# Rewriting a fused convolution-and-mixer kernel: a two-stage odd-frequency DFT with exchanges through DRAM, a row-form mixer with DMA transposes, and one list of tasks

## The chip, the cores and the metric

The kernel runs on one core of one Trainium2 chip. The time is the device time of one execution in microseconds (us); each figure is the median of several executions of the same program. The kernel before took 506.17 us (four runs, 503.19 to 508.12).

The engines are named as the profile names them: PE (TensorE, matmuls), PEld (its weight loads), DVE (VectorE), ACT (ScalarE), POOL (GpSimd) and SP (SyncE, which here issues every DMA). Matmul results land in PSUM; in these kernels DVE or ACT copies ("evicts") them to on-chip memory (SBUF).

## The reference, cut to what matters

Sequence S = 2048, width D = 640, hidden F = 1536, all bf16. Two branches read the same input `x = A_q` and are mixed by a gate per row.

```python
# branch A: a 4-tap causal filter, then a convolution as long as the sequence
k_shift = sum over t of pad(k)[t : t+S] * shift_k[:, 3-t]
kv      = k_shift * v
y       = irfft(rfft(pad(kv)) * rfft(pad(ssm_k)))[:S].astype(bf16)
y       = y + kv * ssm_D
a       = q * y
# branch B: a mixer that moves channel groups in time
h   = gelu(layernorm(x) @ w1)                          # 640 -> 640
h   = 4 groups of 160 channels, moved by 1, -1, 2, -2 rows
x1  = x + h @ w2
b   = x1 + gelu(layernorm(x1) @ w3) @ w4               # 640 -> 1536 -> 640
g   = sigmoid((x * gate_w).sum(-1))
out = g * a + (1 - g) * b
```

## The kernel before

It is four blocks of work, one after the other. (1) Tables of sines are generated on DVE and ACT. (2) The mixer runs in column form: `x` is transposed on its way in from DRAM, channels lie on the partitions, the means of the layernorm come from matmuls with a matrix of ones, and gelu is four operations, two of them on DVE reading PSUM. (3) The filter `k*v` runs on DVE, row block by row block. (4) The long convolution is cut into 4 blocks of 512 rows. Each block is transformed by a dense DFT matrix, every pair of blocks is multiplied on DVE, and each block is transformed back.

```python
NBLK = 4
...
def gelu_to(ps, writes):
    nc.scalar.activation(out=sq[:], in_=ps, func=ACT.Square, scale=float(np.sqrt(GELU_C)))
    nc.vector.scalar_tensor_tensor(out=uu[:], in0=sq[:], scalar=1.0, in1=ps, ...)      # L223
    nc.scalar.activation(out=sg[:], in_=uu[:], func=ACT.Sigmoid, scale=GELU_K)         # L226
    for (oap, r0, cnt) in writes:
        nc.vector.tensor_tensor(out=oap, in0=sg[r0:r0 + cnt], in1=ps[r0:r0 + cnt], op=ALU.mult)  # L228
...
for c in range(SC):                       # mixer, second half: 4 chunks of 512 rows
    X1N = normalize(XT, c)
    for ft in range(FT):                  # 12 tiles of W3, five matmuls each
        ...
        gelu_to(ps[:], [(GT[:, ft, :], 0, P)])
    for uu in range(SUB):                 # W4, plus an identity matmul that adds x1 back
        ...
for u in range(ST):                       # k*v: eight DVE operations of 640 columns per row block
    ...
    for j in (2, 1, 0):
        nc.vector.tensor_tensor(out=tmp[:], in0=KJ[:, j, :], in1=CJ[:, j, :], op=ALU.mult)  # L355
        nc.vector.tensor_tensor(out=acc[:], in0=acc[:], in1=tmp[:], op=ALU.add)             # L356
...
for i in range(NBLK):                     # convolution
    fwd_transform([KV[:, i * LT + tt, :] for tt in range(LT)], XSP[:], 1.0)
    for kblk in range(i, NBLK):
        for qt in range(LT):              # six or eight DVE operations of 128 x 640 each (L393)
            tt_op(t1[:], Xc, Hc, ALU.mult)
            tt_op(t2[:], Xs, Hs, ALU.mult)
            ...
    for m in range(LT):                   # inverse transform (L459), gate, result
        ...
```

Of the kernel before, what the change touches and what calls it, by code (L numbers as in the profile page):

```python
# [13 lines left out]
I32 = mybir.dt.int32  # L14

NBLK = 4
GELU_K = 1.5957691216057308
GELU_C = 0.044715
# [3 lines left out]
def kernel(  # L22
# [17 lines left out]
    P = nc.NUM_PARTITIONS  # L40

    _, S, D = A_q.shape
    Fh = B_w3.shape[1]
    assert S % (NBLK * P) == 0 and D % P == 0 and Fh % P == 0
    ST = S // P
    DT = D // P
    FT = Fh // P
    NCH = min(512, S)
    assert S % NCH == 0
    SC = S // NCH  # L50
    SUB = NCH // P
    L = S // NBLK
    LT = L // P
    M2 = 2 * L
    CG = D // 4
    shifts = [1, -1, 2, -2]
    NF = CG // P
    R = CG % P
    assert R in (0, 32, 64)
    assert 4 * NF * P + 4 * R == D  # L60

    def nchunks(n, c=512):
        res = []
        o = 0
        while o < n:
            w = min(c, n - o)
            res.append((o, w))
            o += w
        return res

    DCH = nchunks(D)

    q2 = A_q.rearrange("b s d -> (b s) d")
    k2 = A_k.rearrange("b s d -> (b s) d")
    v2 = A_v.rearrange("b s d -> (b s) d")
    out2 = out.rearrange("b s d -> (b s) d")

    consts = ctx.enter_context(tc.tile_pool(name="consts", bufs=1))
    persist = ctx.enter_context(tc.tile_pool(name="persist", bufs=1))
    kpool = ctx.enter_context(tc.tile_pool(name="kpool", bufs=1))  # L80

    KV = persist.tile([P, ST, D], BF16, name="KV")
    T2 = persist.tile([P, ST, D], BF16, name="T2")
    G32 = persist.tile([P, ST], F32, name="G32")
    OMG32 = persist.tile([P, ST], F32, name="OMG32")

    DBC = consts.tile([P, D], BF16, name="DBC")
    nc.sync.dma_start(out=DBC[:], in_=A_ssm_D.partition_broadcast(P))
    GWT = consts.tile([P, DT], BF16, name="GWT")
    with nc.allow_non_contiguous_dma(reason="gate weight transpose (tiny)"):  # L90
        nc.sync.dma_start(out=GWT[:], in_=gate_w.rearrange("(dt p) -> p dt", p=P))
    GWC = consts.tile([P, DT], F32, name="GWC")
    nc.vector.tensor_copy(out=GWC[:], in_=GWT[:])
    CJB = consts.tile([P, D * 4], BF16, name="CJB")
    nc.sync.dma_start(out=CJB[:], in_=A_shift_k.rearrange("d j -> (d j)").partition_broadcast(P))
    CJ = consts.tile([P, 4, D], BF16, name="CJ")
    CJBv = CJB.rearrange("p (d j) -> p d j", j=4)
    for j in range(4):
        nc.vector.tensor_copy(out=CJ[:, j, :], in_=CJBv[:, :, j])
    ONES = consts.tile([P, P], BF16, name="ONES")  # L100
    nc.vector.memset(ONES[:], 1.0)
    EPS = consts.tile([P, 1], F32, name="EPS")
    nc.vector.memset(EPS[:], 1e-5)
    CROUND = float(2 ** 23 + 2 ** 22)
    BL = consts.tile([P, 1], F32, name="BL")
    nc.vector.memset(BL[:], float(L))
    BZ = consts.tile([P, 1], F32, name="BZ")
    nc.vector.memset(BZ[:], 0.0)
    BC = consts.tile([P, 1], F32, name="BC")
    nc.vector.memset(BC[:], CROUND)  # L110
    BM = consts.tile([P, 1], F32, name="BM")
    nc.vector.memset(BM[:], -2.0 * M2 * CROUND)

    basis = ctx.enter_context(tc.tile_pool(name="basis", bufs=1))
    FW = basis.tile([P, 2, LT, L], BF16, name="FW")
    SIN_SCALE = np.pi * (1 - 2.0 ** -20) / M2

    def gen_basis(gen_pool, dst, kt, ncols, row_is_t):
        GC = min(ncols, 512)
        irow = gen_pool.tile([P, 1], I32, name="irow")  # L120
        if row_is_t:
            nc.gpsimd.iota(irow[:], pattern=[[1, 1]], base=P * kt, channel_multiplier=1)
        else:
            nc.gpsimd.iota(irow[:], pattern=[[1, 1]], base=2 * P * kt + 1, channel_multiplier=2)
        frow = gen_pool.tile([P, 1], F32, name="frow")
        nc.vector.tensor_copy(out=frow[:], in_=irow[:])
        for col0 in range(0, ncols, GC):
            icol = gen_pool.tile([P, GC], I32, name="icol")
            if row_is_t:
                nc.gpsimd.iota(icol[:], pattern=[[2, GC]], base=2 * col0 + 1, channel_multiplier=0)  # L130
            else:
                nc.gpsimd.iota(icol[:], pattern=[[1, GC]], base=col0, channel_multiplier=0)
            fcol = gen_pool.tile([P, GC], F32, name="fcol")
            nc.vector.tensor_copy(out=fcol[:], in_=icol[:])
            for comp in range(2):
                n1 = gen_pool.tile([P, GC], F32, name="n1")
                nc.vector.tensor_scalar(out=n1[:], in0=fcol[:], scalar1=frow[:], scalar2=float(L if comp == 0 else 0),
                                        op0=ALU.mult, op1=ALU.add)
                qq = gen_pool.tile([P, GC], F32, name="qq")
                nc.vector.tensor_scalar(out=qq[:], in0=n1[:], scalar1=1.0 / (2 * M2), scalar2=CROUND,  # L140
                                        op0=ALU.mult, op1=ALU.add)
                dd = gen_pool.tile([P, GC], F32, name="dd")
                nc.vector.tensor_scalar(out=dd[:], in0=qq[:], scalar1=CROUND, scalar2=float(2 * M2),
                                        op0=ALU.subtract, op1=ALU.mult)
                rr = gen_pool.tile([P, GC], F32, name="rr")
                nc.vector.tensor_tensor(out=rr[:], in0=n1[:], in1=dd[:], op=ALU.subtract)  # L146
                nc.scalar.activation(out=dst[:, comp, kt, col0:col0 + GC], in_=rr[:], func=ACT.Sin, scale=SIN_SCALE)  # L147

    genfw = ctx.enter_context(tc.tile_pool(name="genfw", bufs=1))
    for kt in range(LT):  # L150
        gen_basis(genfw, FW, kt, L, True)

    with ExitStack() as bctx:
        xt_pool = bctx.enter_context(tc.tile_pool(name="xtp", bufs=1))
        stat_pool = bctx.enter_context(tc.tile_pool(name="statp", bufs=2))
        chunk_pool = bctx.enter_context(tc.tile_pool(name="chunkp", bufs=2))
        ep_pool = bctx.enter_context(tc.tile_pool(name="epp", bufs=2))
        ps_mlp = bctx.enter_context(tc.tile_pool(name="psmlp", bufs=4, space=bass.MemoryType.PSUM))
        ps_row = bctx.enter_context(tc.tile_pool(name="psrow", bufs=2, space=bass.MemoryType.PSUM))

        pieces = []
        n0 = 0
        for gi in range(4):
            for f in range(NF):
                pieces.append((n0, P, gi * CG + f * P, shifts[gi]))
                n0 += P
        for gi in range(4):
            if R:
                pieces.append((n0, R, gi * CG + NF * P, shifts[gi]))
                n0 += R  # L170
        assert n0 == D

        XT = xt_pool.tile([P, DT, S], BF16, name="XT")
        for dt in range(DT):
            nc.sync.dma_start_transpose(out=XT[:, dt, :], in_=q2[0:S, dt * P:(dt + 1) * P])  # L175
        RSTD = xt_pool.tile([P, S], BF16, name="RSTD")
        MRR = xt_pool.tile([P, S], BF16, name="MRR")

        def ln_all(srcT):
            varls = []  # L180
            mscs = []
            for c in range(SC):
                ps_sum = ps_mlp.tile([P, NCH], F32, name="ps_sum", tag="mm")
                ps_sq = ps_mlp.tile([P, NCH], F32, name="ps_sq", tag="mm")
                for dt in range(DT):
                    nc.tensor.matmul(ps_sum[:], lhsT=ONES[:], rhs=srcT[:, dt, c * NCH:(c + 1) * NCH],  # L186
                                     start=(dt == 0), stop=(dt == DT - 1))
                for dt in range(DT):
                    sq = stat_pool.tile([P, NCH], BF16, name="sq")
                    nc.scalar.activation(out=sq[:], in_=srcT[:, dt, c * NCH:(c + 1) * NCH], func=ACT.Square)  # L190
                    nc.tensor.matmul(ps_sq[:], lhsT=ONES[:], rhs=sq[:],  # L191
                                     start=(dt == 0), stop=(dt == DT - 1))
# [26 lines left out]
        def gelu_to(ps, writes):  # L219
# [7 lines left out]
            for (oap, r0, cnt) in writes:  # L227
                nc.vector.tensor_tensor(out=oap, in0=sg[r0:r0 + cnt], in1=ps[r0:r0 + cnt], op=ALU.mult)  # L228
# [271 lines left out]
```

## Time and profile before

| | before |
|---|---|
| time, median | 506.17 us |
| span in the profile | 503.0 us |
| PE / DVE / ACT busy | 371 / 414 / 230 us |
| DMA moved | 30.4 MB |

These lines are from the profile's page of the kernel before: the span, the busy time of each engine, the same in 40 equal slices (each digit is a busy share in tenths), the chain of waits that ended last as shares of the span, and two of the costly groups of instructions (line, engine, operation, output<-input, shape, count, then busy us and mean ns of one, then the idle time before them and what ended it).

```profile
span 503.0 us, 6097 instructions
PE 371.2 (74%) x2104; PEld 178.2 (35%) x2104; DVE 414.1 (82%) x987; ACT 230.1 (46%) x381; POOL 19.8 (4%) x33
...
PE   0743376648995489899899998778849692869685
...
DVE  4849699898783797795977959998899999999954
ACT  1777662444479682552734725644416111402301
...
DVE 48%; PE 20%; DMA 13%; ACT 8%; SPq 7%; issue 4%; DVEq 0%; ACTq 0%
...
L226 ACT ACTIVATE gsg<-guu 128x512 bf16<-128x512 bf16 x68 | 42.2, 624 | 12.0 <-DVE guu L223 11.8
...
L355 DVE TENSOR_TENSOR ktmp<-KJ,CJ 128x640 bf16<-128x640 bf16 x48 | 23.8, 496 | 6.3 <-DMA KJ<-in_A_k_dram 5.6
```

DVE is busy 82% of the span and holds 48% of the chain. The DVE row stays at 7 to 9 nearly everywhere, so it is not one stage: it sets the pace in most. But the PE row is not far below it. The two groups show how the work is done: gelu goes back and forth between ACT and DVE (the ACT step waited 12 us in all for DVE), and a DVE operation on 640 bf16 columns takes 0.50 us, 48 times in this one line. The view by windows says the same for two stages; its columns are the window, its length, then busy us (and count) of PE, PEld, DVE, ACT and POOL, the granted PE clock, the DMA share and GB/s. The first line is W3/W4 with `k*v` beside it, the second the spectral products and inverse transforms.

```profile
150.00:310.00 160.00, 140.05 (x844) 70.37 (x843) 123.53 (x249) 88.61 (x149) 0.00 (x0) 0.96 0.22 69
...
357.00:503.00 146.00, 109.19 (x699) 56.60 (x696) 129.27 (x318) 35.90 (x53) 0.55 (x1) 0.86 0.11 34
```

In the W3/W4 stage PE (140 of 160 us) is even busier than DVE (124).

### The profile page before, as it was taken

To read this page: it belongs to the slowest core of one execution; us is meant where nothing else is said; L and a number is where in the kernel's file an instruction comes from. 1 tells how busy PE (TensorE), PEld (TensorE's weight loads), DVE (VectorE), ACT (ScalarE), POOL (GpSimd) and SP (SyncE) were. 2 spreads that over 40 slices of the span, in tenths; PEclk is the share of its full clock that TensorE was granted. 3 is DMA by queue.
4 is the path that set the end of the run, shared out by engine and by line. 5 is a ranking of instruction groups with operands and counts; after the bars stand their busy time and mean duration, and the time that the engine had idled before them with its cause. 6 is when DMAs were issued, how large, how long until landed. Compare 5 with 4: busy or idle time off the path is not lost.

```text
span 503.0 us, 6097 instructions
## 1 busy us (share of the span) xinstructions
PE 371.2 (74%) x2104; PEld 178.2 (35%) x2104; DVE 414.1 (82%) x987; ACT 230.1 (46%) x381; POOL 19.8 (4%) x33
## 2 busy tenths in 40 slices
PE   0743376648995489899899998778849692869685
PEld 0210022224431135445355455334315251425343
DVE  4849699898783797795977959998899999999954
ACT  1777662444479682552734725644416111402301
POOL 3100000000050000000000000100000000000000
PEclk9765596976998699999999999988879798779979
DMA  7932100001284002203024151111203000301201
GB/s 161 203 104 67 52 0 1 1 13 48 84 279 166 0 0 66 66 1 130 2 67 131 27 158 39 39 29 40 52 0 94 13 1 0 106 0 41 66 7 60
DMA packets 45725, 30.36 MB, mean 60 GB/s; under 512 B 28293, under 2 KB 44927, under 8 KB 45695
## 3 DMA queue, kind: packets, MB, share of 16 engines
q1 hardware_dynamic: 45694, 29.98, 20.9%
q8 instruction: 16, 0.26, 0.2%
q14 instruction: 15, 0.11, 0.1%
HBM read 22.11 MB, written 2.62 MB: 49 GB/s over the span
## 4 chain that ended last, share of the span: by engine, by line
DVE 48%; PE 20%; DMA 13%; ACT 8%; SPq 7%; issue 4%; DVEq 0%; ACTq 0%
DMA KJ<-in_A_k_dram 10%; PE psi L459 7%; DVE YSP L393 6%; PE psf L374 5%; DVE GT L228 5%; DVE guu L223 5%; DVE GST L228 4%; DVE ktmp L355 4%; SPq L175 3%; DVE acc L356 3%; ACT sq L190 2%; DMA HB<-in_A_ssm_k_dram 2%; DVE rr L146 2%; SPq L384 1%; DVE XN L215 1%
## 5 line engine op out<-in xcount | busy, mean ns | idle before, releaser
L459 PE MATMUL psi<-YSP,IV 128*128 128x512 bf16 (+1 forms) x448 | 72.6, 324 | 22.3 <-DVE YSP L393 15.5
L374 PEld LDWEIGHTS <-FW 128*128 128x128 bf16 x512 | 41.9, 102 | 58.9 <-issue 23.3
L332 PE MATMUL psr<-W_1158,GT 128*128 128x512 bf16 (+1 forms) x384 | 59.2, 299 | 0.0
L459 PEld LDWEIGHTS <-IV 128*128 128x128 bf16 x448 | 36.6, 103 | 57.9 <-issue 27.8
L374 PE MATMUL psf<-HB,FW 128*128 128x512 bf16 (+1 forms) x256 | 40.8, 318 | 11.3 <-DMA HB<-in_A_ssm_k_dram 11.0
L226 ACT ACTIVATE gsg<-guu 128x512 bf16<-128x512 bf16 x68 | 42.2, 624 | 12.0 <-DVE guu L223 11.8
L374 PE MATMUL psf<-KV,FW 128*128 128x512 bf16 (+1 forms) x256 | 38.8, 314 | 10.2 <-ACT XSP L378 9.4
L321 PEld LDWEIGHTS <-W_1157 128*128 128x128 bf16 x240 | 23.6, 99 | 45.4 <-issue 19.4
L332 PEld LDWEIGHTS <-GT 128*128 128x128 bf16 x384 | 29.9, 98 | 21.8
L191 PE MATMUL ps_sq<-sq,ONES 128*128 128x512 bf16 x40 | 19.1, 494 | 21.8 <-ACT sq L190 21.0
L378 ACT ACTIVATE XSP<-psf 128x640 bf16<-128x640 f32 x32 | 21.9, 701 | 26.4 <-DVE pt_3949 L393 17.0
L378 ACT ACTIVATE HSP<-psf 128x640 bf16<-128x640 f32 x32 | 21.4, 699 | 21.5 <-PE psf L374 21.5
L329 PE MATMUL psr<-IDW,XT 128*128 128x512 bf16 (+1 forms) x160 | 29.6, 299 | 1.0 <-POOL IDW L310 1.0
L190 ACT ACTIVATE sq<-XT 128x512 bf16<-128x512 bf16 x40 | 23.6, 622 | 12.9 <-DMA XT<-in_A_q_dram 12.7
L355 DVE TENSOR_TENSOR ktmp<-KJ,CJ 128x640 bf16<-128x640 bf16 x48 | 23.8, 496 | 6.3 <-DMA KJ<-in_A_k_dram 5.6
L253 PEld LDWEIGHTS <-W1P 128*128 128x128 bf16 x100 | 11.6, 116 | 43.8 <-issue 38.4
L352 DVE TENSOR_TENSOR acc<-KJ,CJ 128x640 bf16<-128x640 bf16 x16 | 7.8, 490 | 21.9 <-DMA KJ<-in_A_k_dram 21.9
L186 PE MATMUL ps_sum<-XT,ONES 128*128 128x512 bf16 x40 | 14.9, 479 | 14.1 <-DMA XT<-in_A_q_dram 14.1
L356 DVE TENSOR_TENSOR acc<-acc,ktmp 128x640 bf16<-128x640 bf16 x48 | 24.4, 507 | 1.0
L147 ACT ACTIVATE IV<-rr 128x512 bf16<-128x512 f32 x16 | 10.1, 630 | 20.7 <-DVE rr L146 18.8
L329 PEld LDWEIGHTS <-XT 128*128 128x128 bf16 x160 | 13.3, 98 | 12.6 <-issue 1.5
L215 DVE TENSOR_TENSOR XN<-tnorm,MRR 128x512 bf16<-128x512 bf16 x40 | 15.6, 417 | 0.1
(755 smaller groups left out, 701.2 us busy)
## 6 DMA issues: line engine op xcount, KB each, us to landing
KJ<-in_A_k_dram SPq DMA_DIRECT2D x15, 640.0 KB, 3.9
VT<-in_A_v_dram SPq DMA_DIRECT2D x16, 160.0 KB, 3.2
XQ<-in_A_q_dram SPq DMA_DIRECT2D x16, 160.0 KB, 2.2
out_dram<-kvd SPq DMA_DIRECT2D x16, 160.0 KB, 1.8
W_1157<-in_B_w_dram SPq DMA_DIRECT2D x1, 1920.0 KB, 7.5
W_1158<-in_B_w_dram SPq DMA_DIRECT2D x1, 1920.0 KB, 13.8
CJB<-in_A_shift_k_dram SPq DMA_DIRECT2D x1, 640.0 KB
W1P<-in_B_w_dram SPq DMA_DIRECT2D x4, 160.0 KB, 3.3
```

The costliest lines, as they stand in the source:

```text
L190: nc.scalar.activation(out=sq[:], in_=srcT[:, dt, c * NCH:(c + 1) * NCH], func=ACT.Square)
L223: nc.vector.scalar_tensor_tensor(out=uu[:], in0=sq[:], scalar=1.0, in1=ps, op0=ALU.add, op1=ALU.mult)
L226: nc.scalar.activation(out=sg[:], in_=uu[:], func=ACT.Sigmoid, scale=GELU_K)
L228: nc.vector.tensor_tensor(out=oap, in0=sg[r0:r0 + cnt], in1=ps[r0:r0 + cnt], op=ALU.mult)
L329: nc.tensor.matmul(psr[:, co:co + cw], lhsT=XT[:, dt, u * P:(u + 1) * P], rhs=IDW[:, dt, co:co + cw], start=(dt == 0), stop=False)
L332: nc.tensor.matmul(psr[:, co:co + cw], lhsT=GT[:, ft, uu * P:(uu + 1) * P], rhs=W4[:, ft, co:co + cw], start=False, stop=(ft == FT - 1))
L355: nc.vector.tensor_tensor(out=tmp[:], in0=KJ[:, j, :], in1=CJ[:, j, :], op=ALU.mult)
L356: nc.vector.tensor_tensor(out=acc[:], in0=acc[:], in1=tmp[:], op=ALU.add)
L374: nc.tensor.matmul(ps[:, co:co + cw], lhsT=FW[:, comp, kt, qt * P:(qt + 1) * P], rhs=src_rows[kt][:, co:co + cw], start=(kt == 0), stop=(k ...
L378: nc.scalar.activation(out=dst[:, comp, qt, :], in_=ps[:], func=ACT.Copy, scale=scale)
L393: nc.vector.tensor_tensor(out=o, in0=i0, in1=i1, op=op)
L459: nc.tensor.matmul(ps[:, co:co + cw], lhsT=lhsT, rhs=rhs[:, co:co + cw], start=(si == 0), stop=(si == len(srcs) - 1))
```

## The change

The intent is to do less arithmetic and to let three engines and the DMA queue work at the same time.

- **Convolution.** Time is written as t1 + 16*t2. A transform over t2 (`step1`, one 128x128 matmul per 512 columns), an exchange through DRAM that regroups the rows, and a second transform over t1 (`step2`) give all frequencies of one long odd-frequency DFT. There is then a single product of two spectra (`product`, three wide DVE operations per group), and the same two steps back (`step3`, exchange, `step4`).
- **Mixer.** It runs in row form. Transposes are DMA transposes from SBUF to SBUF. Gelu is a single ACT operation that evicts PSUM as it goes. The residual of the mixer is added by DVE at eviction instead of by identity matmuls.
- **Order.** Every piece is a task with a wished time. The tasks are sorted by it and emitted in this order, so that W3/W4 matmuls lie between the steps of the convolution.

The diff has 1125 lines. This is its core, with cuts marked and bodies shortened:

```diff
-NBLK = 4
-        def gelu_to(ps, writes):
-            ... Square, scalar_tensor_tensor, Sigmoid, tensor_tensor
-        for i in range(NBLK):
-            fwd_transform(...)            # and 288 DVE operations of 128x640, inverse transforms
+    def step1(name, hf, c, scr, ev):
+        for u in range(2):
+            for b in range(2):
+                PE.matmul(ps[:, b * 512:(b + 1) * 512], lhsT=F1[:, hf * P:(hf + 1) * P], rhs=src[:, o:o + 512], ...)
+            A.copy(out=stg[:, u * 1024:(u + 1) * 1024], in_=ps[:])
+        SP.dma_start(out=scr[hf][:, c * 2048:(c + 1) * 2048], in_=stg[:])        # to DRAM
+    def gather(name, hf, s, scr):                                              # and back, regrouped
+        SP.dma_start(out=ax[:], in_=bass.AP(..., ap=[[D, P], [8 * NT * D, 4], [1, D]]))
+    def step2(name, hf, s, ev): ...                                            # four groups: matmul, ACT copy
+    def product(hf, s):
+        V.tensor_tensor(out=p2[0:64], in0=x[0:64], in1=h[64:128], op=ALU.mult)
+        V.tensor_tensor(out=p2[64:128], in0=x[64:128], in1=h[0:64], op=ALU.mult)
+        V.tensor_tensor(out=h[:], in0=x[:], in1=h[:], op=ALU.mult)
+    def step3(hf, s, ev): ...                                                  # two matmuls per group, ACT copy, store
+    def gin(hf, c): ...                                                        # exchange back through DRAM
+    def h_dma(c):
+        for f in range(4):
+            SP.dma_start_transpose(out=st["HT"][:, f, 4 * c:4 * c + 4, HPAD:HPAD + P], in_=hr[:, f]...)
+        SP.dma_start_transpose(out=st["HM0"]..., in_=hr[:, 4]...)
+    def w3(c, fp):
+        ...                                                                    # ten matmuls into 1024 columns
+        A.activation(out=gt[...], in_=ps[:], func=ACT.Gelu_apprx_tanh)
+    def w4(t1, last): ...                                                      # 24 matmuls, DVE adds to x1
+    def step4(t1, last): ...                                                   # matmuls, then three DVE operations
...
+    add(T0 + 8 * k - 3, lambda hf=hf, s=s: step2("h", hf, s, EV["h2"]))
+    add(T0 + 8 * k + 5, lambda hf=hf, s=s: product(hf, s))
+    add(T0 + 8 * k + 6, lambda hf=hf, s=s: step3(hf, s, EV["g3"]))
+    for c in range(4):
+        for fp in range(6):
+            add(TW + 28 * c + 2 * fp, lambda c=c, fp=fp: w3(c, fp))
+        for i in range(4):
+            add((TS4 + 2 * t1 + 3) if late else TW + 28 * c + 12 + 4 * i, lambda ...: w4(t1, late))
...
+    tasks.sort(key=lambda e: (e[0], e[1]))
```

## The prediction

> **What bounds the kernel now.** The page gives a span of 503 us: DVE busy 414 us (82%), PE 371, ACT 230; DMA moves 30.4 MB. The chain that ended last is DVE 48%, PE 20%, DMA 13%, ACT 8%. VectorE sets the pace in most stages: gelu by hand (two operations from PSUM per tile, 0.69 us each), spectral products (0.40 us each), table generation, k*v (0.50 us each).
>
> **What the change removes.** Matmuls fall from 1272 wide (512 columns) and 752 narrow to 837 and 597 (counted in the build). At the paces of the chain view (0.216 us wide: five W3 matmuls in 1.08 us; narrow about 0.07, by difference) PE needs 328 -> 223 us at full clock. DVE falls from about 930 operations to 287. With traced durations, and for 1280/2560 columns an estimate from the traced 640-column 0.50 us at two elements per cycle (the Trainium skill, "VectorE: DVE Perf Modes", perf-mode tier table; the traced 0.50 us agrees): k*v 64 x 0.83 = 53, products 24 x 1.5 = 36, additions and final products from PSUM 48 x 0.82, the rest about 50: about 180 us.
>
> **What it adds.** ACT takes every eviction: 64 of 1024 columns, 96 of 640 (0.70 us, traced), transposes, squares, gelu: about 200 us. 1.04 us for 1024 columns is an estimate from the Trainium skill, "ScalarE: Activation LUTs", "What ACT_TABLE_LOAD costs" (186 ns + 0.833 ns per element); the traced 0.62 us for 512 and 0.70 for 640 agree. DMA doubles to about 63 MB: spectra go through DRAM (h and x 10.5 MB out and back, the result 5.2), transposes 8 MB. Large loads ran at about 300 GB/s (1.9 MB in 7.5 us, 640 KB in 3.9).
>
> **Why not 224 us.** The work is then balanced (PE 223, ACT 200, DVE 180, DMA about 210), and in-order engines hand results to each other, so stages limit each other:
> - Before the spectral loop: about 25 us until the first gelu; then ACT about 90 us, PE 85, but some 36 MB of DMA (120 us at 300 GB/s), issued by one queue whose transposes take 1 to 3 us each to issue. About 135 us.
> - Spectral loop with W3/W4 in between: PE about 112 us at full clock, ACT 86, DMA 20 MB: about 118 us.
> - Tail: return trip of the last half through DRAM (6 us), then DVE 16 x 2 us and four more evictions: about 40 us.
>
> Sum: **293 us**, 8 in 10 between **258 and 335**. Faster by over 2%: 0.98; within 2%: 0.01; slower: 0.01.
>
> **What would show the steps right.** Page: DVE busy 165 to 210 us, PE 225 to 265, ACT 185 to 220, DMA 58 to 66 MB. DVE no longer leads the chain before the tail; there the chain mixes ACT, PE and DMA. Matmul clock near full in the middle third. First gelu at 20 to 30 us; final stage 35 to 45 us with DVE over 70% busy.
>
> **What would make it wrong.** (a) DMA transposes from on-chip memory, which no run has shown, issue or land far slower than those from DRAM (2.3 us per 512 KB): up to 340 us. (b) The single queue blocks later loads behind waiting stores, starving k*v and the gathers. (c) If the interleaving really hides the handoffs, PE's 223 us plus start and tail give about 260. (d) Two PSUM buffers per stage make PE and ACT alternate: the loop grows to 140 us.

## The result

The changed kernel took **304.46 us** (four runs, 304.12 to 304.84), beside 506.17 us for the kernel before: a ratio of 0.6015 with a 95% interval of 0.5992 to 0.6038. A ratio here is the mean time of one kernel's fast runs over that of the other kernel's fast runs of the same rounds, so it is not quite the ratio of the medians quoted. The result is correct. The prediction was 293 us, within 258 to 335.

The same parts of the profile's page, for the changed kernel:

```profile
span 302.3 us, 3944 instructions
PE 242.2 (80%) x1434; PEld 121.2 (40%) x1434; DVE 176.9 (58%) x344; ACT 179.1 (59%) x284; POOL 28.3 (9%) x31
...
PE   2058858364639888999999999999999999995585
...
DVE  8767969927899876501125234462343724099983
ACT  1999867242626666997868886469793676400000
...
PE 30%; DVE 22%; ACT 13%; SPq 7%; DMA 7%; issue 6%; POOL 1%; ACTq 0%; DVEq 0%; POOLq 0%
...
L596 PE MATMUL ps<-x1t,W 128*128 128x512 bf16 x240 | 59.0, 379 | 0.0
L323 ACT CAST stg<-ps 128x1024 bf16<-128x1024 f32 x40 | 38.4, 1020 | 20.5 <-PE ps L321 10.4
...
L357 DVE TENSOR_TENSOR p<-xs,hs 64x2560 bf16<-64x2560 bf16 x8 | 11.9, 1487 | 33.2 <-ACT xs L348 33.2
...
L437 DVE TENSOR_TENSOR acc<-acc,tmp 128x1280 bf16<-128x1280 bf16 x24 | 19.7, 823 | 0.5
```

DVE lost 237 us of busy time and PE 129. The three rows now have different shapes: PE is at 9 from the 17th slice to the 36th, DVE is high at both ends, and ACT is busy until shortly before the end. So there are three stages, each with its own limit. The view by windows shows them (columns as before):

```profile
0.00:24.30 24.30, 8.62 (x30) 3.77 (x31) 19.21 (x91) 17.31 (x34) 5.70 (x12) 1.00 0.91 245
24.30:72.00 47.70, 29.14 (x220) 17.53 (x220) 35.45 (x74) 27.90 (x59) 4.64 (x3) 0.89 0.86 224
72.00:119.00 47.00, 35.25 (x197) 16.78 (x197) 40.08 (x86) 26.82 (x47) 3.53 (x3) 0.89 0.79 245
119.00:149.00 30.00, 29.63 (x154) 13.80 (x152) 6.42 (x12) 25.64 (x29) 14.45 (x13) 1.00 0.79 263
149.00:257.00 108.00, 106.17 (x651) 52.94 (x650) 43.68 (x34) 77.80 (x115) 0.00 (x0) 1.00 0.54 178
257.00:263.50 6.50, 5.85 (x28) 2.57 (x27) 0.00 (x0) 3.52 (x4) 0.00 (x0) 1.00 0.66 215
263.50:302.30 38.80, 27.48 (x159) 13.81 (x158) 32.02 (x50) 0.15 (x1) 0.00 (x0) 0.81 0.44 151
```

Up to 119 us no engine is full: the DMA engines are busy 79 to 91% of the time and DVE 74 to 85%. From 119 us on PE is full with the first W3/W4 tiles and `step1` of `kv`. From 149 to 257 us PE is busy 106 of 108 us at full clock. At the end DVE is busy 32 of 39 us. In the terms of the prediction's sum:

| stage | predicted | measured | off by |
|---|---|---|---|
| before the spectral loop | 135 | 149 | +14 |
| spectral loop with W3/W4 between | 118 | 108 | -10 |
| return through DRAM, then tail | 40 | 45 | +5 |
| sum | 293 | 302 | +9 |

The cut at 257 us is mine: it counts the return trip (257.0 to 263.5 us) with the tail, as the prediction does. Cut at the first `step4` instead, loop and tail measure 113 and 40 us.

The chain of waits shows how the first stage loses time. In this piece (start in us, duration in us, what) SP issues five transposes of `h`, one after the other (L516, L517). A load of 1.2 KB (`dr`) stands behind them in the same queue, and the first matmul of `step1` (L321) can only start after it:

```profile
63.71 1.20 SPq L516
64.96 1.27 SPq L516
...
68.89 1.26 SPq L517
70.20 1.42 DMA dr<-in_A_ssm_D_dram
71.71 0.49 DVE HT L311
72.24 1.02 PE ps L321 x2
73.29 1.94 ACT stg L323 x2
```

So more than 6 us of this piece are issue time of one queue. The same holds for the stretch before it: from 52.3 to 70.2 us the chain lies on SP's issues alone, ten transposes and ten loads (eight of them pieces of W2), one behind the other. Whether issuing the small load earlier would have been enough to start `step1` sooner was not tried. The timeline of the changed kernel (in brackets the idle time of the engine before it and what ended it) has the price, PE idle for 6.7 us:

```profile
72.24 1.86 PE L321 MATMUL ps<-HT,F 128*128 128x512 bf16 x4 [6.71 <-DVE HT L311]
```

And this is one turn of the chain in the spectral loop: evictions of `step2` on ACT, three products on DVE, `step3`, its eviction, then W4 matmuls that fill in.

```profile
183.78 2.51 ACT xs L348 x4
186.31 1.49 DVE p L357
187.81 1.50 DVE p L358
189.33 1.50 DVE hs L359
190.88 0.45 PE ps L370 x2
191.68 0.70 ACT gs L374
...
193.72 1.53 PE ps L604 x16
```

Two views disagree about the loop. Read alone, the chain says that each turn waits 7 us for ACT and DVE, and that shorter products would pay. The windows say that PE is busy 98% of the loop, which leaves nothing to gain there. The experiments decide between them.

### The profile page after: what moved, and what is told of

Read it like the earlier page. It is cut to its first block, busy times and chain, and to the rows that moved or that the text cites. A ratio compares the mean times of both kernels' runs of the same rounds, so it can differ in the third digit from the quotient of the medians.

```text
span 302.3 us, 3944 instructions
## 1 busy us (share of the span) xinstructions
PE 242.2 (80%) x1434; PEld 121.2 (40%) x1434; DVE 176.9 (58%) x344; ACT 179.1 (59%) x284; POOL 28.3 (9%) x31
## 4 chain that ended last, share of the span: by engine, by line
PE 30%; DVE 22%; ACT 13%; SPq 7%; DMA 7%; issue 6%; POOL 1%; ACTq 0%; DVEq 0%; POOLq 0%
PE ps L604 9%; PE ps L596 8%; ACT xs L348 6%; SPq L516 5%; PE ps L321 3%; DVE hs L359 3%; DVE p L358 3%; DVE p L357 3%; PE ps L370 3%; DVE X L558 3%; ACT gs L374 3%; DVE ot L625 2%; ACT stg L323 2%; PE ps L372 2%; PE ps L346 2%
## 5 line engine op out<-in xcount | busy, mean ns | idle before, releaser
L604 PE MATMUL ps<-W,gt 128*128 128x512 bf16 (+1 forms) x384 | 62.5, 306 | 0.8 <-DVE ot L607 0.8
L596 PE MATMUL ps<-x1t,W 128*128 128x512 bf16 x240 | 59.0, 379 | 0.0
L323 ACT CAST stg<-ps 128x1024 bf16<-128x1024 f32 x40 | 38.4, 1020 | 20.5 <-PE ps L321 10.4
L509 PE MATMUL psm<-WA,xt 128*128 128x512 bf16 (+1 forms) x160 | 30.0, 348 | 20.3 <-DVE WA L455 10.2
L604 PEld LDWEIGHTS <-gt 128*128 128x128 bf16 x384 | 30.2, 99 | 24.8 <-issue 3.7
L596 PEld LDWEIGHTS <-W 128*128 128x128 bf16 x240 | 22.3, 97 | 25.2
L374 ACT CAST gs<-ps 128x640 bf16<-128x640 f32 x32 | 20.6, 695 | 16.7 <-PE ps L372 14.5
L597 ACT ACTIVATE gt<-ps 128x1024 bf16<-128x1024 f32 x24 | 24.6, 1027 | 8.0 <-PE ps L596 7.7
L346 PE MATMUL ps<-ax,TB 128*128 128x512 bf16 (+1 forms) x128 | 26.2, 298 | 0.3
L554 PE MATMUL psw<-WA,HT 128*128 128x512 bf16 (+1 forms) x128 | 22.4, 306 | 4.6 <-DVE X L558 3.6
L321 PE MATMUL ps<-HT,F 128*128 128x512 bf16 x40 | 13.4, 441 | 13.9 <-ACT stg L323 7.2
```

The source lines that it names most:

```text
L321: PE.matmul(ps[:, b * 512:(b + 1) * 512], lhsT=F1[:, hf * P:(hf + 1) * P], rhs=src[:, o:o + 512], start=True, stop=True)
L323: A.copy(out=stg[:, u * 1024:(u + 1) * 1024], in_=ps[:])
L346: PE.matmul(ps[:, o:o + w], lhsT=st["T2"][:, g, :], rhs=ax[:, i, o:o + w], start=True, stop=True)
L374: A.copy(out=gs[:, i % 2, :], in_=ps[:])
L509: PE.matmul(ps[:, o:o + w], lhsT=xt[:, i, k, :], rhs=W1X[:, k, o:o + w], start=(k == 0), stop=(k == DC - 1))
L554: PE.matmul(ps[:, o:o + w], lhsT=h_tile(f, t1), rhs=W2P[:, f, o:o + w], start=(f == 0), stop=(f == 4))
```

## The experiments

The theory: each of the three stages has its own limit. Before the loop it is the issuing and moving of data, in the loop the number of matmuls on PE, in the tail DVE. The rivals: (R1) the loop is limited by the handoffs that the chain lists, or by DMA; (R2) the gain is mostly gelu's move from DVE to ACT, and the rest of the rewrite matters little; (R3) the interleaving is decoration, and the same work in sequence would take about as long.

For the loop I read two times from each trace, both counted from the first matmul of `step2`: to the first matmul of `step4` ("loop"), and to DVE's first final product. The first `step4` matmul needs only the half of the spectrum that came back long before, so "loop" can end before the return trip of the second half does; the final product needs both halves.

| kernel | first step2 | first step4 | loop | to the first final product | PE clock in the loop |
|---|---|---|---|---|---|
| changed kernel | 149.5 | 262.4 | 112.9 | 114.5 | 1.00 |
| products in quarters | 152.1 | 263.6 | 111.5 | 112.2 | 1.00 |
| half of W4 left out | 147.2 | 247.8 | 100.6 | 107.7 | 1.00 |
| 10.5 MB more DMA in the loop | 151.5 | 264.4 | 112.9 | 114.7 | 1.00 |
| fewer transposes before it | 142.4 | 255.3 | 112.9 | 114.4 | 1.00 |
| 5.2 MB more DMA before it | 159.9 | 272.9 | 113.0 | 115.8 | 1.00 |
| W3's gelu by hand | 158.6 | 289.3 | 130.7 | 140.2 | 0.95 |
| no W3/W4 in the loop | 235.7 | 336.3 | 100.6 | 109.1 | 0.76 |

Three of these kernels (the changed one, quartered products, more DMA in the loop) are the same up to the loop, and start it at 149.5 to 152.1 us. So a shift of 3 us between two single traces says nothing.

### 1. b_gelu: the kernel before, with gelu in one ACT operation

```diff
-            ... (three tile allocations)
-            nc.scalar.activation(out=sq[:], in_=ps, func=ACT.Square, scale=float(np.sqrt(GELU_C)))
-            nc.vector.scalar_tensor_tensor(out=uu[:], in0=sq[:], scalar=1.0, in1=ps, op0=ALU.add, op1=ALU.mult)
-            nc.scalar.activation(out=sg[:], in_=uu[:], func=ACT.Sigmoid, scale=GELU_K)
-            for (oap, r0, cnt) in writes:
-                nc.vector.tensor_tensor(out=oap, in0=sg[r0:r0 + cnt], in1=ps[r0:r0 + cnt], op=ALU.mult)
+            for (oap, r0, cnt) in writes:
+                nc.scalar.activation(out=oap, in_=ps[r0:r0 + cnt], func=ACT.Gelu_apprx_tanh)
```

> One part alone: the kernel before with its hand-made gelu (two ScalarE and two VectorE operations per tile) replaced by one ScalarE gelu from PSUM, as the changed kernel has it. If VectorE time comes off the span one for one, some 90 us go and it takes 410 to 420 us. If PE stands right behind VectorE in the W3/W4 stage (its matmuls there need about 130 of 160 us at the warm pace), only 35 to 50 us go: 455 to 472 us. I expect the second.

It took 473.21 us (470.50 to 473.84), a ratio of 0.9311 (0.9266 to 0.9356), and is correct. DVE's busy time fell by 91 us (414.1 to 323.0), but the time only by 35. The W3/W4 part shows why. The view by windows of this kernel, from 144 us to its last W4 matmul:

```profile
144.00:271.40 127.40, 126.39 (x774) 64.81 (x774) 42.99 (x107) 42.02 (x67) 0.00 (x0) 0.98 0.14 45
```

DVE is busy a third of the time (43 us) and PE 126 of 127 us. With DVE relieved, PE was right behind it. R2 falls: gelu alone is worth a sixth of the 202 us gained. The rest needs fewer matmuls and products.

### 2 and 3. a_seq and a_seq2: the changed kernel, with W3/W4 before the loop instead of in it

```diff
-            add(TW + 28 * c + 2 * fp, lambda c=c, fp=fp: w3(c, fp))
+            add(TW + 3 * c + 0.2 * fp, lambda c=c, fp=fp: w3(c, fp))
-            add((TS4 + 2 * t1 + 3) if late else TW + 28 * c + 12 + 4 * i, ...: w4(t1, late))
+            add(TW + 3 * c + 1.2 + 0.4 * i, ...: w4(t1, False))
```

(The last two layernorms, the load of W4 and the last writes move with it.)

> Interleaving undone: W3 and W4 of all four chunks run before the spectral loop instead of inside it; the same instructions. Theory: the loop alone is a chain of hand-offs (evictions, products, next matmuls) of about 85 to 95 us that W3/W4 fill with PE work; undone, their 80 us of PE come on top of it: 345 to 365 us. Rival: the loop is bound by something that interleaving doesn't change (the DMA round trips, ScalarE's evictions): under 320 us.

The fast runs took 377.53, 378.73 and 379.49 us: a ratio of 0.7446 (0.7407 to 0.7485), and correct. That is 74 us more than the changed kernel, where 41 to 61 were expected: I had put W3/W4 at 80 us of PE, and the trace below has them at 110. The one run that was profiled fell in a slow state (480.98 us, PE clock 0.562 over the whole run), so its trace could not be used.

> The same kernel as a_seq, for a trace in the fast state (the profiled run of a_seq had the matmul clock at half). 375 to 382 us if fast. Theory: with W3 and W4 gone from it, the spectral loop (first to last of its matmuls) takes 85 to 100 us against 113 with them inside, at a PE busy share under half, and W3/W4 take their 80 us alone before it.

It took 378.01 us (a single run, so its state is unknown; it agrees with the fast runs above). Its windows are W3/W4 alone, the loop alone, and the tail:

```profile
116.70:234.80 118.10, 115.52 (x677) 57.87 (x677) 20.27 (x31) 45.71 (x51) 14.45 (x13) 1.00 0.26 84
234.80:335.80 101.00, 63.76 (x261) 28.12 (x261) 35.71 (x24) 63.48 (x99) 0.00 (x0) 0.76 0.52 173
335.80:376.20 40.40, 18.48 (x66) 8.02 (x64) 28.66 (x46) 1.07 (x2) 0.00 (x0) 0.54 0.56 187
```

The loop alone takes 101 us with PE busy 64 us of it (63%, where I had expected under half) at three quarters of the clock, and W3/W4 alone, with most of `step1` of `kv` beside them, take 118 us with PE full. Together, in the changed kernel, they cover 143 us (from 119 us to the first `step4`), all but W4's last four tiles, which stand in its tail. Alone, the convolution steps take 101 us because they wait for each other, and the mixer's matmuls fit into these waits. R3 falls: the order is worth 74 us.

The low clock beside an idle PE agrees with the Trainium skill, "TensorE: Matmul & The Clock Gate", Part 1, which says that an idle array drops to half its clock. Here it was 1.00 where PE was full, 0.76 where it was busy 63% of the time and 0.54 where it was busy 46%. Whether the lower clock cost time in the loop was not tested by itself.

### 4. a_prod4: products cut into quarters

```diff
-        V.tensor_tensor(out=p2[0:64], in0=x[0:64], in1=h[64:128], op=ALU.mult)
-        V.tensor_tensor(out=p2[64:128], in0=x[64:128], in1=h[0:64], op=ALU.mult)
-        V.tensor_tensor(out=h[:], in0=x[:], in1=h[:], op=ALU.mult)
+        for i in range(4):
+            V.tensor_tensor(out=p2[0:64, i], in0=x[0:64, i], in1=h[64:128, i], op=ALU.mult)
+            V.tensor_tensor(out=p2[64:128, i], in0=x[64:128, i], in1=h[0:64, i], op=ALU.mult)
+            V.tensor_tensor(out=h[:, i], in0=x[:, i], in1=h[:, i], op=ALU.mult)
```

> The three spectral products of a group cut into four pieces each, so that the next matmuls start after about 1.2 us instead of 4.5 us; same results. Theory (PE streams 103 of the 108 us of the loop): within 4 us of the changed kernel's 304. Rival (the chain of waits through ScalarE's evictions and VectorE's products bounds the loop): 10 to 25 us less.

It took 303.08 us (301.81 to 304.35), a ratio of 0.5961 (0.5928 to 0.5994), and is correct. `step3` can now start after a quarter of the 4.5 us of products that stood in the chain above, in all eight turns. The loop went from 112.9 to 111.5 us. If the handoffs set the pace, some 27 us of products in the chain would have shrunk to about 7. The last `step3` matmul did start sooner (101.5 us after the first of `step2` instead of 106.2), but W3 matmuls that earlier had stood between the steps then ran behind it, and the loop gained 1.4 us. The loop is not bound by the products, although the chain goes through them: it passes through a wait even where another engine would have been full anyway.

### 5. a_w4half: half of W4's matmuls left out

```diff
-            for f in range(FC):
-                PE.matmul(ps[:, o:o + w], ..., start=(f == 0), stop=(f == FC - 1))
+            for f in range(0, FC, 2):
+                PE.matmul(ps[:, o:o + w], ..., start=(f == 0), stop=(f == FC - 2))
```

> Wrong result on purpose: W4 sums over 6 of its 12 inner tiles, 1.7 us of PE less in each of 16 tiles; 9 of them lie in the loop, 3 before it, 2 bare at the end. Theory (PE bounds the loop): 20 to 26 us less, 278 to 284 us. Rival (hand-offs bound it): only the end gets shorter, 4 to 9 us less.

It took 291.97 us (291.51 to 294.10), a ratio of 0.5751 (0.5720 to 0.5781). The values are wrong on purpose; they stayed within the tolerance of the comparison, so it was called correct, which says something about the tolerance and nothing about the kernel. The total fell by 12.5 us, between the two expectations. The trace of the changed kernel has ten W4 tiles in the loop, not the nine of the expectation; half of their matmuls is 60 of each width, some 17 us of PE, an estimate by the pace of the traces (0.216 us for 512 columns, about 0.07 for 128).

The loop to the first `step4` fell by 12.3 us (112.9 to 100.6). But not all of this is gain, as the timeline of this kernel shows: PE reached `step4` before the second half of the spectrum had come back, ran one W4 tile and then stood idle.

```profile
254.38 0.81 PE L616 MATMUL ps<-gin,F 128*128 128x512 bf16 x6 [2.68 <-DMA gin<-S_g]
...
280.76 5.08 PE L604 MATMUL ps<-W,gt 128*128 128x512 bf16 x24 [0.82 <-DVE ot L607]
```

To the first final product the gain is 6.8 us (114.5 to 107.7). Another 3.5 came behind it, mostly because W4's bare matmuls at the very end took 5.1 us instead of 8.7, and 2.3 before the loop. So the loop followed PE, but with less than half of what was taken away. Without any filler it takes 109.1 us to the same point, though at a lower clock. The convolution's own waits may therefore be a floor just below PE's time; no run here separates the two.

### 6. a_dma2: 16 extra copies of 640 KB in the loop

```diff
         st[name, hf, s] = ax
+        jk = dram.tile([P, 4 * D], BF16, name=f"J_{name}{hf}{s}")
+        SP.dma_start(out=jk[:], in_=scr[hf][:, s * 4 * D:(s + 1) * 4 * D])
```

> Beside each of the 16 gathers of the loop, one more copy of the same size between two DRAM buffers (10.5 MB read and written more, inside the loop where DMA is 54% busy). Theory (PE bounds the loop): at most 8 us more. Rival (the DRAM exchange bounds the loop by bandwidth): 25 us more or above.

It took 306.56 us (303.54 to 307.99), a ratio of 0.6028 (0.5974 to 0.6082), and is correct: no difference from the changed kernel that the interval would show. In the loop the DMA engines moved 247 GB/s instead of 178, and the loop stayed at 112.9 us. With experiments 4 and 5 this speaks against R1 for the loop as it stands: PE limits it, not DMA and not the handoffs through DVE's products. ACT's evictions were not tested by themselves, and by experiment 5 the waits of the convolution are not far behind PE, some 7 us.

### 7. a_htrans: two DMA transposes per chunk instead of five

`HT` is laid out by chunk, so that four pieces go in a single DMA.

```diff
-        for f in range(4):
-            SP.dma_start_transpose(out=st["HT"][:, f, 4 * c:4 * c + 4, HPAD:HPAD + P], in_=hr[:, f]...)
+        SP.dma_start_transpose(out=st["HT"][:, c].rearrange("p f a b -> p (f a) b")[:, :, HPAD:HPAD + P],
+                               in_=hr[:, 0:4].rearrange("p f a b -> p (f a b)"))
-        return st["HT"][:, f, u, o:o + P]
+        return st["HT"][:, u // 4, f, u % 4, o:o + P]
```

(The allocation of `HT` and the view for its memsets change with it.)

> Two DMA transposes per chunk of hidden rows instead of five (16 blocks at once instead of four times 4); same bytes, same results. The traced issue cost is 1.26 us for 4 blocks and 3.1 for 20, so about 2.4 us less of the queue per chunk, 10 us in all. Theory (between 52 and 82 us the chain of waits runs through the issue of these transposes): 4 to 9 us less. Rival (the stage waits for DMA bandwidth or VectorE's k*v anyway): within 2 us.

It took 297.47 us (295.97 to 297.56), a ratio of 0.5847 (0.5816 to 0.5878), and is correct. The loop starts 7.1 us earlier and takes the same 112.9 us, so the whole gain lies before it. The issue times on SP, from the view of one line's instructions (duration in ns: least, median, most), first of the changed kernel and then of this one:

```profile
L516 SPq DMA_TRANSPOSE HT<-hr x16: 1201/1264/2054, 32.9 to 79.7; - x16
```

```profile
L515 SPq DMA_TRANSPOSE HT<-hr x4: 2003/3405/3665, 33.5 to 69.1; - x4
```

Four transposes of four 128x128 blocks each take 5.1 us to issue, one of sixteen blocks takes 3.4. Over four chunks that is 6.6 us, about the size of the gain.

### 8. a_tail: the tail's work moved from DVE to ACT (a first attempt)

```diff
-        V.tensor_scalar(out=gq[:], in0=st["q2"][:, t1 % 2, :], scalar1=GS[:, t1:t1 + 1], ...)
-        V.tensor_tensor(out=gq[:], in0=ps[:], in1=gq[:], op=ALU.mult)
+        A.activation(out=gq[:], in_=ps[:], func=ACT.Copy, scale=GS[:, t1:t1 + 1])
+        V.tensor_tensor(out=gq[:], in0=st["q2"][:, t1 % 2, :], in1=gq[:], op=ALU.mult)
-            V.scalar_tensor_tensor(out=ot[:], in0=X1[:, t1, :], scalar=OMG[:, t1:t1 + 1], in1=gq[:], ...)
+            V.tensor_tensor(out=ot[:], in0=X1[:, t1, :], in1=gq[:], op=ALU.add)
```

(`x1` is multiplied by 1 - g earlier, W4's additions to it scale by the same factor, and W4's last four tiles come among the first pieces of `step4` instead of partly at the end.)

> The tail moved off VectorE: ScalarE (idle there) evicts the last transform with the gate as its scale, the other gate factor is multiplied in earlier, VectorE keeps two bf16 operations of 0.45 us per tile instead of 2.0 us, and the last four W4 tiles are added before the final products. Theory (the tail is bound by VectorE, 32 of 39 us busy, plus 9 us in which the last two W4 tiles run bare): 12 to 18 us less. Rival (the loads of the spectra and the stores of the result bound it): under 5 us less.

It took 300.86 us (300.35 to 301.47), a ratio of 0.5921 (0.5892 to 0.5950), and is correct. This gained 3.6 us where I had expected far more. DVE's work in the tail did fall, from 32 to 19 us, but the tail (from the first `step4` on) only from 40 to 36. The timeline of this kernel (start, us, engine, line, operation, count, and in brackets the idle time before it and what ended it) shows new waits:

```profile
288.06 0.79 ACT L625 ACTIVATE gq<-ps,GS 128x640 bf16<-128x640 f32 x1 [1.35 <-DVE ot L629]
...
290.02 1.10 DVE L629 TENSOR_TENSOR ot<-X,gq 128x640 bf16<-128x640 bf16 x2 [0.65 <-DMA out_dram<-ot]
...
293.04 1.01 DVE L629 TENSOR_TENSOR ot<-X,gq 128x640 bf16<-128x640 bf16 x2 [0.42 <-DMA out_dram<-ot]
```

ACT waits until DVE frees one of two `gq` buffers, and DVE waits until a store has landed and frees one of two `ot` buffers. So in the second half of this tail the limit moved from DVE's busy time to the number of buffers. In the first half (264 to 281 us in the same timeline) it is the order: PE runs one W4 tile of 3.4 us after another between the pieces of `step4`, and ACT waits 2.2 to 3.0 us for each piece.

### 9. a_tail2: the same, with four buffers and W4's tiles spread out

```diff
-            add(TS4 + 2 * t1 - 20 if c == 3 else TW + ..., lambda t1=t1: w4(t1, False))
+            add(TS4 + 6 * i + 5 if c == 3 else TW + ..., lambda t1=t1: w4(t1, False))
-        gq = ring.tile([P, D], BF16, name="gq", tag="gq", bufs=2)
+        gq = pool("T").tile([P, D], BF16, name="gq", tag="gq", bufs=4)      # q2 and ot likewise
```

(The diff is against experiment 8.)

> As a_tail (which gave 4 us, not 12 to 18), with the last four W4 tiles spread between the final products, and four buffers instead of two for the loaded q, the product and the output. In the trace of a_tail four W4 tiles in a row kept the last transforms from PE for 14 us, and then each tile waited for a buffer or for a load issued behind a waiting store. Theory (order and buffers held it, not the engines): 9 to 15 us less than the changed kernel's 304. Rival (the stores and loads bound the tail): still 299 or more.

It took 292.18 us (291.78 to 292.94), a ratio of 0.5759 (0.5730 to 0.5789), and is correct. Now 12.3 us are gained. How much of that belongs to the buffers and how much to the order was not tested apart. Its tail reads:

```profile
261.00:290.00 29.00, 22.78 (x162) 12.36 (x160) 18.12 (x36) 13.07 (x17) 0.00 (x0) 0.94 0.64 216
```

PE, at 23 of 29 us, is now the busiest engine of the tail, and its clock is 0.94 where it was 0.81. Part of the old tail had been waste at its very end. The timeline of the changed kernel shows 8.7 us of bare W4 matmuls there, which began only when DVE freed a PSUM buffer:

```profile
288.90 0.89 DVE L607 SCALAR_TENSOR_TENSOR ot<-ps,OMG,X 128x640 bf16<-128x640 f32 x1
289.85 8.74 PE L604 MATMUL ps<-W,gt 128*128 128x512 bf16 x48 [0.82 <-DVE ot L607]
```

### 10. a_handgelu: the changed kernel, with W3's gelu by hand again

```diff
-        A.activation(out=gt[...], in_=ps[:], func=ACT.Gelu_apprx_tanh)
+        A.activation(out=gv, in_=ps[:], func=ACT.Square, scale=float(np.sqrt(0.044715)))
+        V.scalar_tensor_tensor(out=gv, in0=gv, scalar=1.0, in1=ps[:], op0=ALU.add, op1=ALU.mult)
+        A.activation(out=gv, in_=gv, func=ACT.Sigmoid, scale=1.5957691216057308)
+        V.tensor_tensor(out=gv, in0=gv, in1=ps[:], op=ALU.mult)
```

> One part undone in the changed kernel: W3's gelu made by hand again, two ScalarE and two VectorE operations of 1024 columns (about 1.0 and 1.2 us each) in place of one. It adds 58 us to VectorE and 25 us to ScalarE, most of it in the loop, where VectorE is 44 and ScalarE 78 of 108 us busy. If the slack of the two engines takes it up (PE bounds the loop): under 312 us. If the longer chain of four operations on two PSUM buffers holds PE up: 318 to 340 us. I expect the second.

It took 341.74 us (338.26 to 342.86), a ratio of 0.6719 (0.6661 to 0.6777), and is correct: 37 us more, just above the 318 to 340 us that I expected. Stage by stage it lost 9 us before the loop, 18 in it and 11 after it. The same edit, for W3 alone, costs here as much as it brought in the old kernel for W1 and W3 together. There PE stood right behind DVE. Here PE was the limit of the loop and lost its place: it is busy 111 of 130.7 us. Of the 19 us in which it is idle there, it waits 9.9 for DVE's last gelu operation (L601) and 4.5 for the products on DVE. That this comes from the longer hold on each PSUM buffer (two ACT and two DVE operations instead of one ACT) is my reading, not tested by itself.

### 11. a_predma: eight extra copies of 640 KB before the loop

```diff
+    for n in range(8):
+        add(6.1 + 4 * n, lambda n=n: extra(n))      # SP.dma_start(out=jk[:], in_=q_rows[:, 4*(n%4):4*(n%4)+4, :])
```

> Eight more copies of 640 KB between DRAM buffers, spread over the stage before the spectral loop (5.2 MB read and written; that stage moves 36 MB in 149 us with DMA 79 to 91% busy). Their issue alone costs the queue some 3.5 us (0.43 us each in the trace). If that stage is bound by the order and the cost of issues, as the gain of the merged transposes suggests: 2 to 7 us more. If it is bound by bandwidth, as the prediction's 36 MB at 300 GB/s had it: 15 us more or above.

It took 316.95 us (314.48 to 318.28), a ratio of 0.6240 (0.6202 to 0.6278), and is correct: 12.5 us more, between the two expectations. The loop starts 10.4 us later. Issuing the eight copies took SP about 4 us in all (0.5 us each), and 5.2 MB at the 259 GB/s of this stage would be 20 us (an estimate from these two numbers). So the stage is bound by neither alone: there is some slack in bandwidth, and more is lost than the issue time. The exact split between issue order and bandwidth stays open.

### 12. a_best3: experiments 4, 7 and 9 together

> a_htrans, a_tail2 and a_prod4 together. If the stages follow one another and don't overlap, the gains add: 7.5 from the transposes, 9 to 15 from the tail, 1 from the products: 281 to 288 us. If the start's gain is given back in the loop, above 290.

It took **281.37 us** (280.37 to 282.60), a ratio of 0.5546 (0.5514 to 0.5578), and is correct. It beats both kernels: 7.6% under the changed one by medians. The gains of its parts were 1.4, 7.0 and 12.3 us, 20.7 in sum; together they gave 23.1. They lie in three different stages, which is why they add up. Its windows, before the loop, in it and after it:

```profile
0.00:140.00 140.00, 100.33 (x601) 50.80 (x602) 108.99 (x274) 98.12 (x168) 28.54 (x31) 0.95 0.89 251
140.00:251.60 111.60, 109.89 (x675) 55.44 (x673) 55.38 (x106) 80.20 (x117) 0.00 (x0) 1.00 0.61 195
251.60:279.60 28.00, 22.59 (x161) 12.33 (x159) 18.11 (x36) 12.95 (x17) 0.00 (x0) 0.94 0.63 201
```

What is left is PE in the loop, and the first half, where no engine is full and the DMA engines are busy 89% of the time.

## Why the prediction was right

The total was right: 304 us against 293, inside the range. That it came so near is partly luck: +14 and +5 us in two stages stand against -10 in the third. The steps, one by one:

- **Amount of work.** DVE was predicted at about 180 us (check range 165 to 210) and was busy 176.9. PE was predicted at 223 us at full clock, which at the mean granted clock of 0.94 makes 237 (check range 225 to 265), and was busy 242.2. DMA had 58 to 66 MB and moved 62.5. Counting operations and multiplying by traced durations gave these three totals within a few per cent, across a rewrite that left almost no line standing. **ACT was a miss**: I said about 200 us (check range 185 to 220) and it was busy 179.1. Each wide eviction was sized well (1.02 and 0.70 us), but operations that follow each other overlap in the trace: the 160 of them kept ACT busy 124 us, not the 134 of the sum. The rest of ACT's work, which I had not listed, was 55 us where 66 were left for it.
- **Durations scaled from the Trainium skill.** "VectorE: DVE Perf Modes", perf-mode tier table, has bf16 products between SBUF operands at twice the plain rate, and at the plain rate with PSUM. I had put 0.83 us on 1280 columns and 0.82 on 640 columns from PSUM; the trace has 0.823 and 0.82. "ScalarE: Activation LUTs", section "What ACT_TABLE_LOAD costs", gives 186 ns + 0.833 ns per element, so 1.04 us for 1024 columns; the trace has 1.020. Both agree.
- **Before the loop: 135 us predicted, 149 measured. This is the term that was mis-sized most.** I had summed the bytes (36 MB, 120 us at 300 GB/s) and added 15 us for issue. The 300 did not follow from the two loads that the prediction names: 1.97 MB in 7.5 us is 262 GB/s, and 0.66 MB in 3.9 us is 168. At 262 the same sum gives 137 + 15 = 152 us. The stage moved its 36 MB at about 242 GB/s; that is bytes over time, and does not say by itself what held the stage. Merging transposes gave 7 us back (experiment 7), and extra bytes cost about half of what bandwidth alone would say (experiment 11). Issue time of transposes on the single queue is therefore a shown part of the stage's time. The remainder is not split.
- **Loop: 118 us predicted, 108 measured.** I had PE at 112 us and 6 us of friction on top. There was hardly any to pay: PE was busy 106 of the 108 us, and experiments 4 and 6 show neither the products nor DMA in its way. At the pace of back-to-back matmuls its matmuls come to about 104 us (403 wide at 0.216 and 248 narrow at 0.07, an estimate).
- **Tail: 40 us predicted, 45 measured.** The return trip took 6.5 us (6 predicted), and DVE was busy 32 us, 83% of the rest and 71% of the whole, as the check required (over 70%). The excess lies at the very end: 8.7 us of bare W4 matmuls, held back by a PSUM buffer, for which DVE waited 3.5 us. I had counted operations there, not buffers, and experiment 8 repeats the same mistake.
- **Checks on the page.** The first gelu came at 24.3 us (predicted 20 to 30); the matmul clock was 1.00 in the middle third; DVE fell from 48% to 22% of the chain. "DVE no longer leads the chain before the tail" holds for the loop. It fails for a stretch before it: from 83 to 118 us the chain runs through `k*v` and the W2 additions on DVE, which is busy 40 of 47 us there.
- **What would have made it wrong.** (a) Transposes from on-chip memory far slower than those from DRAM: not so. Sixteen 128x128 blocks took 3.4 us to issue and landed after 5.8 (experiment 7); from DRAM, in the kernel before, they took 2.4 and 5.0. Splitting them cost 7 us, far from the way to 340. (b) A queue that blocks later loads: partly so. The 1.2 KB load stood behind the issue of five transposes, and between 75 and 155 us the queue waited 29 us in all at the stores of `step1` (L326) until ACT had filled them. Which loads that delayed, and how much of the first stage's excess it is, was not tested. (c) 260 us if the interleaving hides all handoffs: it hides them in the loop, but the other two stages stayed long. (d) PE and ACT alternating on two PSUM buffers: did not happen, the loop is full.

One thing the prediction did not say is how much depends on the order. The same operations in sequence take 378 us. Operation counts alone would not have told the two apart.

## What to carry to other kernels

Size a rewrite stage by stage, with the largest of PE, DVE, ACT, bytes and issue time in each; here three of four totals came within a few per cent, and the largest error sat in the stage where no engine is full. A chain of waits says where the last-ended work passed, not what a shorter step is worth: look first whether some engine is full over the same stretch, and if one is, take work from that engine, and expect to meet the next limit soon (experiment 5 got back less than half of what it took out). Put the matmuls of an independent computation between the steps of a latency-bound one (74 us here), and after relieving an engine ask at once which engine, buffer or queue stands right behind it: in the old kernel 56 of the 91 us that DVE saved never reached the time, and in the first attempt at the tail most of 13 us did not.

## What the Trainium skill lacked or had wrong

- "DMA: Bandwidth & Descriptors" gives issue costs of a transposing DMA only as the comparison column of a table for another chip, and that table does not give the size of a tile. On this chip, issuing a DMA transpose held the queue for 1.26 us for four 128x128 bf16 blocks (SBUF to SBUF), 3.4 us for sixteen and 3.1 to 7.6 us for twenty, while a plain 640 KB load held it for about 0.4. For a kernel with one queue this was the part worth knowing: 7 us of 304.
- "VectorE: DVE Perf Modes", perf-mode tier table, has no row for `scalar_tensor_tensor`. All in bf16 and in SBUF, 640 columns took 885 ns, no less than 820 ns with PSUM as an input, while a plain `tensor_tensor` in SBUF took 0.49 us. Applying its scalar elsewhere and using a plain addition was part of experiments 8 and 9, not tested by itself.
- No page gives the time of the accumulated output of an ACT or DVE operation: the trace shows an extra reading instruction of 190 to 205 ns on ACT and 84 ns on DVE after each.
- No page gives the time of a power on GpSimd: 128x4 elements took 1.29 us, and it stood on the chain before the normalization.
- The start of the skill ("Trainium Kernel Development and Optimization", section "Performance Expectations") calls matmul busy time a bad metric of distance to the roofline. This case agrees (a 512-column matmul of W3 is recorded at 379 ns, but five follow each other in 1.08 us), yet busy time was the right view for the question which engine a stage is bound by: 106 of 108 us.
- "TensorE: Matmul & The Clock Gate", Part 1, tells of clocks that change within microseconds, and of a low clock that stuck for 50 us and more. One execution here, of the kernel that otherwise takes 378 us, kept a low clock far longer: from 24 us on, all 38 remaining slices of its page stand at 0.5, the mean is 0.562, and it took 481 us. I found no page that says what causes that, and no run here shows it.
